# Linear attention and two feed-forward blocks on one core: clamps of the decays of seven tiles move to GpSimd, eight copies into the state move to ScalarE

## The chip, the cores and the metric

The kernel runs on one core of a Trainium2 chip. A core has five engines with a queue of instructions each: TensorE (PE in the profile, with its weight loads as PEld), VectorE (DVE), ScalarE (ACT), GpSimd (POOL) and SyncE (SP), which here issues the transfers. An engine takes its instructions strictly in the order in which they were written for it. The metric is device time in microseconds (us) of one launch.

## The reference

Batch 4, 8 heads, 768 steps, head size 48, all float32. The result of the attention, laid out as 3072 tokens by 384, goes through two feed-forward blocks.

```python
for t in range(S):
    cur = einsum('bhd,bhe->bhde', u * k[t], v[t])
    y[t] = einsum('bhd,bhde->bhe', r[t], state + cur)
    state = w[t][..., None] * state + einsum('bhd,bhe->bhde', k[t], v[t])
x = y laid out as (batch*step, heads*48)
h = x @ w_in;  x = (h * clip(h + 3, 0, 6) / 6) @ w_out            # d_ff 2048
h = x @ w_in2; s = h * softmax(h); x = layernorm(s) * g @ w_out2  # d_ff 1024
```

The decays `w` lie between 0.80 and 0.95 in the inputs. The kernel clamps them to 0.75 to 1.25 and checks on the side that none lay outside.

## The kernel before

**Tiles.** The 768 steps are cut into six chunks of 128, and a chunk of one batch is a tile: 24 tiles, numbered chunk times 4 plus batch. Tiles 0 to 3 are the first chunk. Each tile goes through six stages. `stw` clamps the decays (`wc <- w`, L451, 128x496 elements) and, on ScalarE, sums how far they lie outside. `st0` transposes `wc` and `r` on TensorE into `wt` and `rt` (L434) and runs products over time on VectorE (scans L478 and L484; `e <- rt,e`, L488). `st1` transposes `k` into `kt` and multiplies (`q <- kt,q`, L506), while GpSimd forms `z = r*k*u` (L508, L509). `st2` transposes `q` (`ktp`, L520), forms the products `pa` (L535), masks them into `am` (L543, L544, L550 for tiles 0 to 3; L553, L557 later) and sums `z` into `d` (L560 or L529). `st3` forms `kv` (L572), the tile's addition to the state, and `yt` (L582 for tiles 0 to 3; L589, L595 later), then writes the state: for tiles 0 to 3 two copies of `kv` into `s_st` (L607, 48 partitions x 192 elements each), later a sum (L605). `st4` splits the result into a high and a low part (`xh`, L641; `xl`, L642).

**PSUM.** `wt`, `rt`, `kt`, `ktp`, `pa`, `kv` and `yt` share three buffers. A matmul into a buffer waits until the last reader of what lay there is done.

**Feed-forward.** When tiles 0 to 3 are through, the first feed-forward block starts on their 512 columns in 16 slots, one for each 128 of the 2048 inner columns: 9 matmuls into `h` (L660), Relu on ScalarE (L664), a product on VectorE (`t`, L665), the high part `gh` (L666), the low part `gl` (L668, on GpSimd for the first group of 16 slots) and 9 matmuls into `y` (L680). While the first 16 slots run, VectorE also decodes the weights of each slot: five instructions on 128x768 elements (L40, L43, L50, L53, and L61 for the low part `w_l`), with two on ScalarE (L44, L60). Tiles 4 to 8 are worked in the same stretch, one for every four slots. Then the block goes through its five other groups, and the second block follows.

**Order.** For tiles 0 to 3 the order on SP and GpSimd is that of the program's text. On the other engines, and everywhere later, a scheduler sets it when the program is built, so that an edit can move instructions that it doesn't name. From tile 10 on the decays are clamped in another layout on GpSimd (L447, 128x704 elements).

Of the kernel before, what the change touches and what calls it, by code (L numbers as in the profile page):

```python
# [12 lines left out]
ACTF = mybir.ActivationFunctionType  # L13
ALU = mybir.AluOpType
# [5 lines left out]
W_LO, W_HI = 0.75, 1.25  # L20
# [247 lines left out]
def fast_path(  # L268
# [14 lines left out]
    nc = tc.nc  # L283
# [47 lines left out]
        out=causal.bitcast(F32), in_=ones, pattern=[[1, P]], compare_op=ALU.is_gt, fill=0.0, base=0,  # L331
# [96 lines left out]
    def ps_tile(nm):  # L428
        return ps_a.tile([P, 4, P], F32, tag="pa", name=nm)
# [6 lines left out]
    def stw(i):  # L436
        a = at[i]
        if i >= LATE:
            x = late["w"][:, :, 0:4 * D - 16]
            junk = atp.tile([P, HP, 4 * D - 16], mybir.dt.uint8, tag="junk", name="junk", bufs=1)  # L440
            nc.scalar.activation(
                out=junk, in_=x, func=ACTF.Relu, scale=-1.0, bias=b_lo, accum_out=chk[:, 3 * i:3 * i + 1]
            )
            nc.scalar.activation(
                out=junk, in_=x, func=ACTF.Relu, bias=b_hi, accum_out=chk[:, 3 * i + 1:3 * i + 2]
            )
            nc.gpsimd.tensor_scalar(out=x, in0=x, scalar1=W_HI, scalar2=W_LO, op0=ALU.min, op1=ALU.max)  # L447
            return
        wc = atp.tile([P, H, 64], F32, tag="wc", name="wc", bufs=1)
        flat = slice(0, H * 64 - 16)  # L450
        nc.vector.tensor_scalar(  # L451
            out=wc.rearrange("p h d -> p (h d)")[:, flat], in0=a["w"].rearrange("p h d -> p (h d)")[:, flat],
            scalar1=W_LO, scalar2=W_HI, op0=ALU.max, op1=ALU.min,
        )
        a["wc"] = wc
        junk = atp.tile([P, H, D], BF16, tag="junk", name="junk", bufs=1)
        nc.scalar.activation(
            out=junk, in_=a["w"][:, :, 0:D], func=ACTF.Relu, scale=-1.0, bias=b_lo, accum_out=chk[:, 3 * i:3 * i + 1]
        )
        nc.scalar.activation(  # L460
            out=junk, in_=a["w"][:, :, 0:D], func=ACTF.Relu, bias=b_hi, accum_out=chk[:, 3 * i + 1:3 * i + 2]
        )
# [102 lines left out]
    def st3(i):  # L565
        a = at[i]
        g, b = divmod(i, B)
        vv = a["v"].rearrange("p h d -> p (h d)")
        if g < NG - 1:
            kv = ps_tile("kv")  # L570
            for hp in range(HP):
                nc.tensor.matmul(  # L572
                    out=kv[0:DP, hp, 0:2 * D], lhsT=a["ktok"][:, hp, :], rhs=vv[:, hp * 2 * D:(hp + 1) * 2 * D],
                    start=True, stop=True,
                )
        y = ps_tile("yt")
        yf = y.rearrange("p h t -> p (h t)")[:, 0:DM]
        for hp in range(HP):
            if g == 0:
                for j in range(2):  # L580
                    h = 2 * hp + j
                    nc.tensor.matmul(  # L582
                        out=yf[:, h * D:(h + 1) * D], lhsT=a["am"][j][:, hp, :], rhs=vv[:, h * D:(h + 1) * D],
                        start=True, stop=True,
                    )
                continue
            for j in range(2):
                if g > 0:
                    nc.tensor.matmul(  # L589
                        out=y[64 * j:64 * j + D, hp, :], lhsT=a["sp"][0:DP, hp, j * D:(j + 1) * D],  # L590
                        rhs=a["e"][0:DP, hp, :], start=True, stop=False,
                    )
            for j in range(2):
                h = 2 * hp + j
                nc.tensor.matmul(  # L595
                    out=y[64 * j:64 * j + D, hp, :], lhsT=vv[:, h * D:(h + 1) * D], rhs=a["am"][j][:, hp, :],
                    start=(g == 0), stop=True,
                )
        if g < NG - 1:
            for j in range(2):  # L600
                o, f = 64 * j, D * j
                dst = s_st[b][o:o + D, :, f:f + D]
                src = kv[o:o + D, :, f:f + D]
                if g > 0:
                    nc.vector.tensor_tensor(out=dst, in0=src, in1=a["sp"][o:o + D, :, f:f + D], op=ALU.add)  # L605
                else:
                    nc.vector.tensor_copy(out=dst, in_=src)  # L607
        ys = atp.tile([P, HP, C], F32, tag="ys", name="ys", bufs=1)
        if g == 0:
            ys = ys.rearrange("p h t -> p (h t)")[:, 0:DM]  # L610
            nc.vector.tensor_tensor(out=ys, in0=yf, in1=a["av"].rearrange("p h d -> p (h d)"), op=ALU.add)
            a["ys"] = ys
            return
        for j in range(2):
            o = 64 * j
            nc.scalar.activation(out=ys[o:o + D], in_=y[o:o + D], func=ACTF.Copy)
            nc.sync.dma_start(out=x1d[i, :, j].rearrange("h d t -> d h t"), in_=ys[o:o + D])
        xf = atp.tile([P, KD, C], F32, tag="xf", name="xf")
        nc.sync.dma_start(
            out=xf, in_=x1d[i].rearrange("h j d t -> (h j d) t").rearrange("(c p) t -> p c t", p=P)  # L620
        )
        a["xf"] = xf

    def st4(i):
# [17 lines left out]
        eng.tensor_tensor(out=xl[:, :, sl], in0=xf, in1=xh[:, :, sl].bitcast(F32), op=ALU.subtract)  # L642

    stages = [stw, st0, st1, st2, st3, st4]


# [295 lines left out]
```

## Time and profile before

| | us |
|---|---|
| three runs | 813.21, 817.16, 818.41 (median 817.16) |
| the profiled execution: time | 813.55 |
| the profiled execution: span from first to last instruction | 811.8 |
| busy in the span: PE, DVE, ACT, POOL | 771.9, 539.6, 354.2, 264.5 |

Times in rows of the trace are from the span's start; a row of the timeline gives start, length, engine, line, operation, tiles out and in, shapes, and in brackets how long the engine had been idle and what ended that. Instructions of an engine overlap at their ends, so that starts lie somewhat closer than lengths. "TENSOR_TENSOR_SCAN" in the trace is the scan that the order of the program calls SCALAR_TENSOR_TENSOR on L478 and L484.

### The profile page before, as it was taken

The page shows a single profiled execution, that of the slowest core. Times are in us where ns is not written, and L with a number is a line of the kernel's source. Part 1 is how long each engine was busy: PE and PEld are TensorE (multiplying, and loading weights), DVE is VectorE, ACT ScalarE, POOL GpSimd, SP SyncE. Part 2 cuts the span into 40 slices and gives each one's busy share as a digit, 9 for nine tenths or more (in the row PEclk, how much of TensorE's full clock was granted, in tenths as well). Part 3 has the DMA queues.
Part 4 walks back from the last instruction along what each step waited for, and adds up shares of the span by engine and source line. Part 5 has one row for each costly group of instructions (what it writes and reads, how often), then busy time and mean ns, then how long its engine had stood idle before and what let it go on. Part 6 is the DMA issues. An engine that isn't in the chain of part 4 may idle for free.

```text
span 811.8 us, 12303 instructions
## 1 busy us (share of the span) xinstructions
PE 771.9 (95%) x4390; PEld 649.3 (80%) x4390; DVE 539.6 (66%) x1032; ACT 354.2 (44%) x651; POOL 264.5 (33%) x349
## 2 busy tenths in 40 slices
PE   5799888989999999999999999998999999999996
PEld 5697666668888888888888887886889999999996
DVE  5859999956666666667666663899275545555452
ACT  3325455434444544454444433554354434444342
POOL 4235635655333333333332330223032222222210
PEclk9558999999999999999999999999999999999999
DMA  9844664346444544445333212432111111111100
GB/s 183 148 92 123 157 173 136 87 94 146 101 101 101 139 101 100 101 118 117 86 80 111 71 51 61 140 102 77 39 49 40 47 43 40 45 43 42 37 21 34
DMA packets 155750, 72.56 MB, mean 89 GB/s; under 512 B 91808, under 2 KB 150304, under 8 KB 155680
## 3 DMA queue, kind: packets, MB, share of 16 engines
q1 hardware_dynamic: 153088, 66.98, 33.5%
q10 hardware_dynamic: 2592, 4.72, 1.6%
q8 instruction: 36, 0.59, 0.3%
q14 instruction: 34, 0.28, 0.1%
HBM read 58.30 MB, written 13.37 MB: 88 GB/s over the span
## 4 chain that ended last, share of the span: by engine, by line
PE 69%; DVE 5%; issue 2%; ACT 1%; DMA 1%; POOL 0%; ACTq 0%; SPq 0%; POOLq 0%; DVEq 0%
PE y L680 18%; PE h L660 17%; PE po L878 12%; PE h L851 12%; PE pt L865 3%; PE pa L535 2%; PE yt L589 2%; PE yt L595 2%; DVE dec L50 1%; PE kv L572 1%; DVE dec L53 1%; DVE t L665 1%; DMA raw<-in_moe_w_in_dram 1%; DVE raw L43 1%; PE ktp L520 1%
## 5 line engine op out<-in xcount | busy, mean ns | idle before, releaser
L665 DVE SCALAR_TENSOR_TENSOR t<-t,h 128x512 f32<-128x512 f32 x96 | 65.6, 683 | 101.7 <-ACT t L664 101.5
L664 ACT ACTIVATE t<-h,three 128x512 f32<-128x512 f32 x96 | 65.5, 682 | 133.5 <-PE h L660 133.3
L660 PE MATMUL h<-xh,w_h 128*128 128x512 f32 x288 | 114.9, 400 | 5.5 <-DVE t L665 4.1
L660 PE MATMUL h<-xh,w_l 128*128 128x512 f32 x288 | 113.9, 395 | 6.3 <-DVE w_l L61 6.2
L680 PE MATMUL y<-gh,w_h 128*128 128x512 f32 x288 | 117.2, 407 | 0.6 <-ACT gh L666 0.5
L680 PE MATMUL y<-gl,w_h 128*128 128x512 f32 x288 | 113.7, 395 | 2.5 <-POOL gl L668 2.5
L660 PE MATMUL h<-xl,w_h 128*128 128x512 f32 x288 | 113.4, 394 | 1.0 <-POOL xl L642 1.0
L680 PE MATMUL y<-gh,w_l 128*128 128x512 f32 x288 | 113.1, 393 | 0.0
L666 ACT ACTIVATE gh<-t 128x512 fp32r<-128x512 f32 x96 | 60.7, 632 | 82.7 <-DVE t L665 82.2
L553 POOL TENSOR_TENSOR am<-ident,d 128x512 f32<-128x512 f32 x40 | 50.1, 1271 | 108.0 <-PE yt L595 100.7
L660 PEld LDWEIGHTS h<-xh,w_h 128*128 128x128 f32 x288 | 54.5, 190 | 21.4 <-DVE t L665 6.6
L67 DVE TENSOR_REDUCE nm<-h 128x1 f32<-128x1024 f32 x24 | 29.4, 1225 | 62.6 <-PE h L851 62.5
L660 PEld LDWEIGHTS h<-xh,w_l 128*128 128x128 f32 x288 | 54.2, 188 | 21.0 <-DVE w_l L61 9.6
L668 DVE TENSOR_TENSOR gl<-t,gh 128x512 fp32r<-128x512 f32 x80 | 57.8, 722 | 18.8 <-ACT gh L666 17.4
L680 PEld LDWEIGHTS y<-gh,w_h 128*128 128x128 f32 x288 | 54.3, 188 | 16.7 <-issue 3.1
L878 PE MATMUL po<-w_oh,qh 128*128 128x384 f32 x192 | 67.0, 349 | 0.3 <-ACT qh L867 0.3
L680 PEld LDWEIGHTS y<-gl,w_h 128*128 128x128 f32 x288 | 54.3, 188 | 14.7 <-POOL gl L668 3.7
L878 PE MATMUL po<-w_oh,ql 128*128 128x384 f32 x192 | 65.2, 339 | 0.1
L878 PE MATMUL po<-w_ol,qh 128*128 128x384 f32 x192 | 65.0, 339 | 0.0
L660 PEld LDWEIGHTS h<-xl,w_h 128*128 128x128 f32 x288 | 54.3, 189 | 12.5 <-POOL xl L642 1.5
L680 PEld LDWEIGHTS y<-gh,w_l 128*128 128x128 f32 x288 | 54.2, 188 | 11.5
L867 ACT ACTIVATE qh<-pt 128x512 fp32r<-128x512 f32 x48 | 26.1, 595 | 79.0 <-PE pt L865 79.0
(128 smaller groups left out, 1600.4 us busy)
## 6 DMA issues: line engine op xcount, KB each, us to landing
raw<-in_moe_w_in_dram SPq DMA_DIRECT2D x24, 384.0 KB, 3.4
raw<-in_moe_w_out_dram SPq DMA_DIRECT2D x24, 384.0 KB, 4.0
r<-in_r_dram SPq DMA_DIRECT2D x24, 192.0 KB, 3.8
k<-in_k_dram SPq DMA_DIRECT2D x24, 192.0 KB, 4.1
v<-in_v_dram SPq DMA_DIRECT2D x24, 192.0 KB, 3.1
y1d<-ye ACTq DMA_DIRECT2D x18, 256.0 KB, 2.6
y<-y1d SPq DMA_DIRECT2D x24, 192.0 KB, 2.7
out_dram<-os SPq DMA_DIRECT2D x24, 192.0 KB, 1.9
```

The source lines that it names most:

```text
L67: nc.vector.tensor_reduce(out=nm, in_=h, axis=AX.X, op=ALU.max, negate=True)
L553: nc.gpsimd.tensor_tensor(out=am, in0=ident.unsqueeze(1).to_broadcast([P, HP, C]), in1=dv[:, hh, :].unsqueeze(2).to_broadcast([P, HP, C]), ...
L660: nc.tensor.matmul(out=h, lhsT=a, rhs=b, start=(j == 0), stop=(j == len(ops) - 1))
L664: nc.scalar.activation(out=t, in_=h, func=ACTF.Relu, bias=three)
L665: nc.vector.scalar_tensor_tensor(out=t, in0=t, scalar=6.0, in1=h, op0=ALU.min, op1=ALU.mult)
L666: nc.scalar.activation(out=gh, in_=t, func=ACTF.Copy)
L668: eng.tensor_tensor(out=gl, in0=t, in1=gh.bitcast(F32), op=ALU.subtract)
L680: nc.tensor.matmul(out=y_ps[g][c], lhsT=a, rhs=b, start=(m == 0 and j == 0), stop=(m == M1 - 1 and j == 2))
L851: nc.tensor.matmul(out=h[:, fs], lhsT=a[:, c, :], rhs=b_[:, c, fs], start=(j == 0), stop=(j == len(ops) - 1))
L865: nc.tensor.transpose(out=pt[:, j, :], in_=a["q"][:, m * P:(m + 1) * P], identity=ident)
L867: nc.scalar.activation(out=qh[:, ms, :], in_=pt, func=ACTF.Copy)
L878: nc.tensor.matmul(out=po, lhsT=x[:, m, :], rhs=y[:, m, :], start=(n == 0), stop=(n == 3 * M2 - 1))
```

## The change

The clamp of tiles 3 to 9 goes from VectorE to GpSimd (its two operations are swapped, to the order that the clamp of tiles 10 on has). The copies of the first chunk's `kv` into the state go from VectorE to ScalarE.

```diff
-        nc.vector.tensor_scalar(
+        eng = nc.vector if i < 3 else nc.gpsimd
+        eng.tensor_scalar(
             out=wc.rearrange("p h d -> p (h d)")[:, flat], in0=a["w"].rearrange("p h d -> p (h d)")[:, flat],
-            scalar1=W_LO, scalar2=W_HI, op0=ALU.max, op1=ALU.min,
+            scalar1=W_HI, scalar2=W_LO, op0=ALU.min, op1=ALU.max,
         )
...
                 if g > 0:
                     nc.vector.tensor_tensor(out=dst, in0=src, in1=a["sp"][o:o + D, :, f:f + D], op=ALU.add)
                 else:
-                    nc.vector.tensor_copy(out=dst, in_=src)
+                    nc.scalar.activation(out=dst, in_=src, func=ACTF.Copy)
```

The lines after the first hunk are one higher in the changed kernel. The scheduler also places other instructions anew, up to the end of the stretch with the decodes; three places follow. On VectorE, from the scan `e` of tile 2 to `q <- kt,q` of that tile (`dec` and `raw` are the weights' decode, pa_359 the products of tile 1), there stood before:

```order
L484 SCALAR_TENSOR_TENSOR e<-wt,e,ones 112x127 x4
L43 TENSOR_SCALAR raw<-raw 128x768
L488 TENSOR_TENSOR e<-rt,e 112x512
L50 SCALAR_TENSOR_TENSOR dec<-dec,raw 128x768
L451 TENSOR_SCALAR wc<-w 128x496
L53 SCALAR_TENSOR_TENSOR dec<-raw,dec 128x768
L40 TENSOR_SCALAR dec<-raw 128x768
L550 TENSOR_TENSOR am<-pa_359,causal 128x512
L61 TENSOR_TENSOR w_l<-dec,w_h 128x768
L43 TENSOR_SCALAR raw<-raw 128x768
L560 TENSOR_REDUCE d<-z 128x8
L506 TENSOR_TENSOR q<-kt,q 112x4x128
```

and in the changed kernel:

```order
L485 SCALAR_TENSOR_TENSOR e<-wt,e,ones 112x127 x4
L50 SCALAR_TENSOR_TENSOR dec<-dec,raw 128x768
L489 TENSOR_TENSOR e<-rt,e 112x512
L53 SCALAR_TENSOR_TENSOR dec<-raw,dec 128x768
L40 TENSOR_SCALAR dec<-raw 128x768
L551 TENSOR_TENSOR am<-pa_359,causal 128x512
L43 TENSOR_SCALAR raw<-raw 128x768
L61 TENSOR_TENSOR w_l<-dec,w_h 128x768
L507 TENSOR_TENSOR q<-kt,q 112x4x128
```

The clamp of tile 3 is gone, and the first L43 and the reduce (L560) stand earlier, where the two copies of tile 0 and the first L40 had stood. On VectorE around `ys` of tile 3 (L611, the last of its L611 rows), before:

```order
L451 TENSOR_SCALAR wc<-w 128x496
L550 TENSOR_TENSOR am<-pa_516,causal 128x512
L61 TENSOR_TENSOR w_l<-dec,w_h 128x768
L642 TENSOR_TENSOR xl<-px,xh 128x3x128
L607 COPY s_st_122<-kv 48x4x48 x2
L611 TENSOR_TENSOR ys<-yt,av 128x384
L50 SCALAR_TENSOR_TENSOR dec<-dec,raw 128x768
L529 TENSOR_REDUCE d<-z 128x8
L642 TENSOR_TENSOR xl<-px,xh 128x3x128
L53 SCALAR_TENSOR_TENSOR dec<-raw,dec 128x768
```

and in the changed kernel:

```order
L530 TENSOR_REDUCE d<-z 128x8
L551 TENSOR_TENSOR am<-pa_516,causal 128x512
L50 SCALAR_TENSOR_TENSOR dec<-dec,raw 128x768
L643 TENSOR_TENSOR xl<-px,xh 128x3x128
L612 TENSOR_TENSOR ys<-yt,av 128x384
L53 SCALAR_TENSOR_TENSOR dec<-raw,dec 128x768
L530 TENSOR_REDUCE d<-z 128x8
L643 TENSOR_TENSOR xl<-px,xh 128x3x128
```

One L50 and one reduce have moved from behind `ys` of tile 3 to ahead of it. On GpSimd at the end of the stretch with the decodes (`am` of tile 8, `z` of tile 9), before:

```order
L668 TENSOR_TENSOR gl<-t,gh 128x512
L553 TENSOR_TENSOR am<-ident,d 128x512 x2
L508 TENSOR_TENSOR z<-r,k 128x384
L399 MEMSET late_w 32x4x16 x2
L399 MEMSET late_r 32x4x16 x2
L399 MEMSET late_k 32x4x16 x2
L509 TENSOR_TENSOR z<-z,u_bc 128x384
L668 TENSOR_TENSOR gl<-t,gh 128x512
L502 TENSOR_TENSOR sp<-s_st_116,q 112x384
L668 TENSOR_TENSOR gl<-t,gh 128x512
L642 TENSOR_TENSOR xl<-xf,xh 128x3x128
```

and in the changed kernel:

```order
L669 TENSOR_TENSOR gl<-t,gh 128x512
L554 TENSOR_TENSOR am<-ident,d 128x512 x2
L509 TENSOR_TENSOR z<-r,k 128x384
L399 MEMSET late_w 32x4x16 x2
L399 MEMSET late_r 32x4x16 x2
L399 MEMSET late_k 32x4x16 x2
L510 TENSOR_TENSOR z<-z,u_bc 128x384
L452 TENSOR_SCALAR wc<-w 128x496
L669 TENSOR_TENSOR gl<-t,gh 128x512
L503 TENSOR_TENSOR sp<-s_st_116,q 112x384
L643 TENSOR_TENSOR xl<-xf,xh 128x3x128
L669 TENSOR_TENSOR gl<-t,gh 128x512
```

The clamp of tile 9 stands right ahead of a `gl`, and `xl` ahead of the next `gl`.

## Rows read from the trace of the kernel before

**Rows 1.** Windows: stretch, its length, busy us (instructions) by engine, granted clock, DMA.
```profile
40.00:60.00 20.00, 19.31 (x96) 18.13 (x95) 11.52 (x22) 6.22 (x14) 7.48 (x14) 0.50 0.40 90
...
80.00:100.00 20.00, 17.82 (x100) 13.36 (x100) 19.69 (x31) 10.62 (x19) 11.99 (x11) 1.00 0.63 165
...
160.00:180.00 20.00, 16.79 (x90) 12.29 (x85) 12.17 (x26) 9.05 (x17) 12.69 (x18) 0.91 0.44 102
180.00:200.00 20.00, 20.00 (x136) 16.68 (x135) 11.94 (x25) 8.46 (x15) 10.83 (x12) 1.00 0.59 139
```
**Rows 2.** Timeline of VectorE, 26 to 36 us (start, length, engine, line, operation).
```profile
26.43 0.54 DVE L43 TENSOR_SCALAR raw<-raw 128x768 int32<-128x768 int32 x1
...
28.35 0.42 DVE L451 TENSOR_SCALAR wc<-w 128x496 f32<-128x496 f32 x1
...
30.01 0.69 DVE L550 TENSOR_TENSOR am<-pa,causal 128x512 f32<-128x512 f32 x1
...
31.94 0.55 DVE L560 TENSOR_REDUCE d<-z 128x8 f32<-128x384 f32 x1
...
35.47 0.36 DVE L607 COPY s_st<-kv 48x192 f32<-48x192 f32 x1
```
**Rows 3.** Timeline of TensorE, 30 to 36 us.
```profile
30.75 1.10 PE L434 MATMUL rt<-ident,r 128*112 128x128 f32 x4 [0.51 <-DVE am L550]
...
33.15 1.81 PE L572 MATMUL kv<-v,ktok 128*112 128x96 f32 x8 [1.29 <-DVE q L506]
...
35.97 3.62 PE L582 MATMUL yt<-v,am 128*128 128x48 f32 x16 [1.01 <-POOL q L476]
```
**Rows 4.** Timeline of ScalarE, its shortest copy out of PSUM.
```profile
54.55 0.49 ACT L641 ACTIVATE xh<-px 128x384 fp32r<-128x384 f32 x1 [0.47 <-PE px L637]
```
**Rows 5.** Timeline of VectorE, 59 to 60 us.
```profile
59.42 0.56 DVE L611 TENSOR_TENSOR ys<-yt,av 128x384 f32<-128x384 f32 x1 [2.65 <-PE yt L582]
59.90 0.95 DVE L50 SCALAR_TENSOR_TENSOR dec<-dec,raw 128x768 int32<-128x768 int32 x1
```
**Rows 6.** Groups of VectorE, 60 to 165 us: count, busy us, mean ns, idle before.
```profile
L61 DVE TENSOR_TENSOR w_l<-dec,w_h 128x768 fp32r<-128x768 f32 x14 | 15.9, 1139 | 0.0
L53 DVE SCALAR_TENSOR_TENSOR dec<-raw,dec 128x768 int32<-128x768 int32 x14 | 15.7, 1121 | 0.0
L50 DVE SCALAR_TENSOR_TENSOR dec<-dec,raw 128x768 int32<-128x768 int32 x14 | 13.9, 992 | 0.0
L40 DVE TENSOR_SCALAR dec<-raw 128x768 f32<-128x768 f32 x13 | 12.5, 959 | 0.0
...
L43 DVE TENSOR_SCALAR raw<-raw 128x768 int32<-128x768 int32 x13 | 9.8, 753 | 0.0
...
L451 DVE TENSOR_SCALAR wc<-w 128x496 f32<-128x496 f32 x4 | 4.5, 1130 | 0.1
```
**Rows 7.** Timeline of GpSimd, two instructions between 105 and 117 us.
```profile
105.29 1.27 POOL L668 TENSOR_TENSOR gl<-t,gh 128x512 fp32r<-128x512 f32 x1 [3.93 <-ACT gh L666]
...
116.11 1.29 POOL L668 TENSOR_TENSOR gl<-t,gh 128x512 fp32r<-128x512 f32 x1
```
**Rows 8.** Timeline of VectorE, what started beside those two.
```profile
105.35 1.48 DVE L451 TENSOR_SCALAR wc<-w 128x496 f32<-128x496 f32 x1
...
116.57 1.65 DVE L53 SCALAR_TENSOR_TENSOR dec<-raw,dec 128x768 int32<-128x768 int32 x1
```
**Rows 9.** Timeline of GpSimd, the clamp of tile 10.
```profile
179.36 0.78 POOL L447 TENSOR_SCALAR late_w<-late_w 128x704 f32<-128x704 f32 x1 [0.43 <-ACT junk L444]
```
**Rows 10.** Timeline, GpSimd and TensorE at 169 to 171 us.
```profile
169.34 1.27 POOL L668 TENSOR_TENSOR gl<-t,gh 128x512 fp32r<-128x512 f32 x1
...
170.66 0.51 PE L680 MATMUL y<-gl,w_h 128*128 128x512 f32 x1 [1.98 <-POOL gl L668]
```
**Rows 11.** Timeline of TensorE, 16 matmuls `yt` at either clock.
```profile
18.75 1.96 PE L582 MATMUL yt<-v,am 128*128 128x48 f32 x16 [1.01 <-DVE s_st L607]
...
46.34 3.54 PE L582 MATMUL yt<-v,am 128*128 128x48 f32 x16
```

## The prediction

> **What bounds the kernel now.** I read the windows first, to see which engine limits which stretch, then the timelines of the engines around every instruction that the change names, then the groups of VectorE with their mean lengths.
>
> In the windows [rows 1] the reader is to see three kinds of stretch. From 180 us on TensorE is busy 20.00 of 20 us: nothing that VectorE or GpSimd is spared there makes the end earlier. From 80 to 100 us VectorE is busy 19.69 of 20 us and TensorE only 17.82: here VectorE is the limit, and the stretch, which begins when `ys` of tile 3 has been computed at 59.42 us [rows 5], lasts until TensorE takes over again in the window from 160 us. From 40 to 60 us TensorE is busy 19.31 us, but at a granted clock of 0.50, so at the lower level of 1.2 GHz: that stretch is a chain of tiles 1 to 3 through TensorE. Before it, up to 36 us, TensorE waits for VectorE. So a gain can come from three places: the chain up to 36 us, VectorE's work behind 59.42 us, and the hand-over to TensorE at 160 to 176 us. What is gained in them is kept, because TensorE's work behind them is fixed.
>
> **The chain of the first tiles.** Three rows of TensorE name what ended its waits [rows 3]. `rt` of tile 3 waited 0.51 us for `am` of tile 1, whose reader frees the buffer. `kv` of tile 1 waited 1.29 us for `q` of tile 2 (L506), for the same reason. `yt` of tile 1 waited 1.01 us; the profile puts it down to a memset of GpSimd, but in the order of the program that row needs the two copies of `kv`, and the second of them ended at 35.47 + 0.36 = 35.83 us [rows 2, 3].
>
> On VectorE the new order takes out of the way to `am` the clamp of tile 3 (0.42 us) and an L43 (0.54 us, which goes into the place that the first L40 had, which in turn takes the place of two copies) [rows 2]. The two are 0.96 us by their lengths, some 0.77 by their starts. On the way to `q` the reduce goes too, 0.55 us or 0.47 by starts [rows 2]: together 1.24 us. `kv` of tile 1 waited 1.29 us, so all 1.24 us can be used; `rt` ahead of it, with the 0.51 us that it waited, ends early enough: 30.24 + 1.10 = 31.34 us, against 33.15 - 1.24 = 31.91 us.
>
> The copies then run on ScalarE. No row shows a copy of 48x192 elements there. The nearest one has twice the elements and takes 0.49 us [rows 4]; the other end is what VectorE needs, 0.36 us [rows 2]. Two of them take 0.72 to 0.98 us behind the end of `kv`, against 0.87 us on VectorE (34.96 to 35.83 us), so I count no difference, with 0.15 us to either side. Behind `yt` TensorE hardly waits until 59 us [rows 1], and so the lead reaches `ys` of tile 3 whole: **-1.2 us** (-0.8 to -1.4). The clamp of tile 3 on GpSimd lies in front of a masking instruction that waits for ScalarE anyway, and tile 4's clamp is not needed before the feed-forward begins: nothing, unless `w` lands late.
>
> **Work taken from behind 59.42 us.** VectorE waited 2.65 us for `yt` of tile 3 just before its `ys` [rows 5]. The new order puts one L50 (0.95 us [rows 5]) and one reduce (0.55 us [rows 2]) ahead of that wait, which hides them; by starts that is 1.35 us less in the stretch where VectorE is the limit: **-1.35 us** (0, if their inputs come too late and they hold up `ys`, to -1.5).
>
> **The clamps in that stretch.** Four of the seven lie in it. They took 4.5 us, 1130 ns each [rows 6], but 0.42 us where GpSimd was idle [rows 2]. The reason is to be seen at 105 us: `gl` ran on GpSimd from 105.29 to 106.56 us, and the clamp that started at 105.35 us ended at 106.83 us, about its own length after that [rows 7, 8]. At 116 us an L53 did the same: 1.65 us, against a mean of 1121 ns over all 14 that includes several such waits [rows 6 to 8]. So VectorE and GpSimd hold each other up, and the wait that a clamp no longer has falls to the L50 that stands behind it. I count as saved only the bare 0.4 us, 1.6 us in all.
>
> On GpSimd a clamp costs 0.55 us if its length goes with its elements (0.78 us for 704 of them, and 496 here), and at most 0.78 us [rows 9]. In that time it holds VectorE up if a decode instruction is next. Those make 67.8 of the 105 us [rows 6], or 65%, so a clamp gives back about 0.65 x 0.55 = 0.36 us, and all four 1.4 us. What is left is **-0.2 us**. The ends: -4.5 us, if the waits go with the clamps, and 4 x (0.78 - 0.40) = +1.5 us, if each new clamp holds VectorE up for all of its 0.78 us.
>
> The Trainium skill (Perfetto Trace Analysis, Optimizing Scalar/DVE Operations) warns that the two engines share a port, so that moving work between them might not help, and SBUF — State Buffer (Who interferes with whom) says that the one that comes second waits for the whole of the other's instruction. The rows at 105 and 116 us agree with a wait to the other's end; by that rule alone the four clamps would be worth between nothing and the upper end just given, and the sum would be 1.7 us worse than mine.
>
> **The hand-over.** TensorE waited 1.98 us for the `gl` at 169.34 us [rows 10]. In the new order the clamp of tile 9 stands right ahead of that `gl`, behind the same `z`: **+0.55 us** (0 to 0.78). Its removal from VectorE brings nothing there.
>
> **Sum.** -1.2 - 1.35 - 0.2 + 0.55 = -2.2 us; with the ends of all terms, -7.4 to +1.5 us. Against the profiled execution's own time of 813.55 us this is 811.3 us. That execution lies 3.6 us below the median of the three runs, 817.16 us; the four lie at 813.21, 813.55, 817.16 and 818.41 us, with a median of 815.4 us, and I set the forecast from there: **813.2 us**.
>
> **The rivals.** (1) *Nothing.* The lead of the first tiles is lost, for example because TensorE's rise to the full clock comes no earlier and VectorE fills the time with waits at `ys`. TensorE's 19.31 busy us of 20 speak against it, since a chain without gaps passes a lead on; the many instructions that the scheduler moved speak for it. 815.4 us. (2) *The waits go with the clamps.* VectorE loses all 4.5 us of them, and the other terms stand: 815.4 - 4.5 - 1.2 - 1.35 + 0.55, about 809 us. For it: GpSimd has 8 of 20 us free [rows 1]. Against it: the L50 behind. (3) *Slower: the collisions grow.* In the stretch up to 165 us each of four clamps costs VectorE its whole 0.78 us for the 0.40 it saves, and each also shifts GpSimd's later work onto one more decode instruction, with a wait like that of the L53, 1.65 us less the 0.95 us of an undisturbed L50 of the same size, 0.70 us [rows 5, 8]: 4 x (0.38 + 0.70) = +4.3 us, and 0.78 at the hand-over, against -2.55: +2.5 us, 818 us. It decides once VectorE waits more than 0.6 us longer per tile than now. (4) *The clock.* From 40 to 60 us the granted clock is 0.50 [rows 1], and 16 matmuls `yt` take 3.54 us there and 1.96 us at the full clock [rows 11]. If the shorter waits let TensorE have the full clock for half of the 23 us from 36 to 59 us, that is 11.5 x 0.45 = -5.2 us more, about 808 us. The chain was busy there without a rise, which speaks against it.
>
> **How the numbers follow.** Forecast 0.43, nothing 0.18, waits gone 0.17, collisions grow 0.15, clock 0.07. The range leaves out most of the clock's case and the far ends of the second and third: 807 to 820 us. A difference under 1%, 8.2 us, can hardly be told from none. Faster than 809.0 us is half of the second case and most of the fourth, 0.13; slower than 825.3 us is only a far end of the third, 0.03; within 1% is 0.84.
>
> **What would show it.** In the profile of the changed kernel: `yt` of tile 1 starting near 34.7 us and `ys` of tile 3 near 58.2 us; the wait of VectorE ahead of that `ys` shorter, with an L50 in front of it; GpSimd's clamps at 0.5 to 0.8 us; the decode instructions of 60 to 165 us with the same sum of lengths, within 2 us; TensorE's wait for `gl` near 168 us of 2 to 2.5 us; and from there on the same rows, 2 us earlier. I am wrong if `ys` of tile 3 is not earlier, if the decode instructions get shorter by what the clamps had waited, or if a wait for `wc` from GpSimd shows on TensorE or on VectorE's scans.

## The result and the profile after

The changed kernel takes 807.05 us (four runs, 803.79 to 807.63) against 816.52 us for the kernel before beside it (four runs): ratio 0.9901, 95% interval 0.9872 to 0.9930 (as recorded; the two medians alone would give 0.9884). Timed again later with twelve runs it had 0.9927 (0.9902 to 0.9952). So it gains some 6 to 9 us, where the forecast of 813.2 us, made against 815.4 us, had a gain of 2.2.

In the profile the span is 6.2 us shorter (before 811.8), and TensorE's busy time hardly changed (before 771.9). These are two lines of the page of the changed kernel:

```profile
span 805.6 us, 12307 instructions
PE 772.5 (96%) x4390; PEld 656.2 (81%) x4390; DVE 531.4 (66%) x1017; ACT 355.9 (44%) x659; POOL 275.9 (34%) x356
```

The span is TensorE's busy time plus its idle time, so the gain is idle time: 811.8 - 771.9 = 39.9 us before, 805.6 - 772.5 = 33.1 us after. The windows tell where. Columns as in [rows 1]:

```profile
40.00:60.00 20.00, 19.87 (x99) 18.70 (x99) 9.69 (x16) 7.62 (x18) 10.59 (x17) 0.50 0.46 89
...
80.00:100.00 20.00, 16.81 (x107) 13.47 (x107) 19.97 (x33) 10.89 (x20) 12.82 (x10) 0.91 0.63 159
...
160.00:180.00 20.00, 19.52 (x130) 15.94 (x128) 11.70 (x23) 8.89 (x18) 11.99 (x19) 1.00 0.44 99
180.00:200.00 20.00, 20.00 (x130) 16.80 (x130) 12.34 (x24) 7.36 (x14) 7.15 (x8) 1.00 0.57 137
```

From 160 to 180 us TensorE is idle for 0.48 us and was for 3.21 us [rows 1]: this one window holds 2.7 of the 6.8 us. By the same view the rest is 1.8 us up to 60 us and 2.2 us from 60 to 160 us.

**The first tiles.** The timeline of TensorE, answering [rows 3]:

```profile
31.98 1.06 PE L434 MATMUL rt<-ident,r 128*112 128x128 f32 x4
33.95 1.81 PE L573 MATMUL kv<-v,ktok 128*112 128x96 f32 x8 [0.91 <-DVE q L507]
36.56 3.62 PE L583 MATMUL yt<-v,am 128*128 128x48 f32 x16 [0.80 <-ACT s_st L608]
```

The three waits fell from 0.51, 1.29 and 1.01 us to 0, 0.91 and 0.80 us. Still `yt` starts 0.59 us later than before. In this execution TensorE was at the lower clock, 1.2 GHz, already in `yt` of tile 0 (3.62 us, where [rows 11] has 1.96). On VectorE, answering [rows 5]:

```profile
54.88 1.34 DVE L50 SCALAR_TENSOR_TENSOR dec<-dec,raw 128x768 int32<-128x768 int32 x1
...
59.98 0.56 DVE L612 TENSOR_TENSOR ys<-yt,av 128x384 f32<-128x384 f32 x1 [3.28 <-PE yt L583]
60.45 0.95 DVE L53 SCALAR_TENSOR_TENSOR dec<-raw,dec 128x768 int32<-128x768 int32 x1
```

The L50 stands ahead of `ys` and there is still a wait of 3.28 us: it was hidden, as forecast.

**The decode stretch.** Groups of VectorE from 60 to 165 us, answering [rows 6]:

```profile
L61 DVE TENSOR_TENSOR w_l<-dec,w_h 128x768 fp32r<-128x768 f32 x14 | 18.1, 1294 | 1.8 <-ACT w_h L60 1.8
L53 DVE SCALAR_TENSOR_TENSOR dec<-raw,dec 128x768 int32<-128x768 int32 x14 | 15.4, 1101 | 0.0
L50 DVE SCALAR_TENSOR_TENSOR dec<-dec,raw 128x768 int32<-128x768 int32 x13 | 13.4, 1031 | 0.1
...
L43 DVE TENSOR_SCALAR raw<-raw 128x768 int32<-128x768 int32 x13 | 9.7, 744 | 0.0
L40 DVE TENSOR_SCALAR dec<-raw 128x768 f32<-128x768 f32 x13 | 8.9, 687 | 0.0
```

The clamps' 4.5 us are gone. The five decode lines sum to 65.5 us against 67.8, with one L50 fewer: but for that L50, 1.3 us shorter, within the 2 us that the forecast allowed. The waits moved among them, from L40 (959 to 687 ns) to L61 (1139 to 1294 ns). On GpSimd the clamps take 0.60 to 1.19 us (the forecast: 0.5 to 0.8). The 0.60 us at 62.50 us stand beside an L40 of VectorE that took 0.83 us (0.55 at 107.10 us), the 1.19 us at 105.12 us beside an L50 that took 1.53 us. Two lines of GpSimd's timeline:

```profile
62.50 0.60 POOL L452 TENSOR_SCALAR wc<-w 128x496 f32<-128x496 f32 x1 [0.20 <-PE wt L434]
...
105.12 1.19 POOL L452 TENSOR_SCALAR wc<-w 128x496 f32<-128x496 f32 x1
```

VectorE is through with the last decode, the 16th L61, earlier than the forecast's terms for this stretch allow, but can't use it. Before, and then after:

```profile
163.06 0.94 DVE L61 TENSOR_TENSOR w_l<-dec,w_h 128x768 fp32r<-128x768 f32 x1
164.03 0.69 DVE L665 SCALAR_TENSOR_TENSOR t<-t,h 128x512 f32<-128x512 f32 x1
```

```profile
157.21 1.23 DVE L61 TENSOR_TENSOR w_l<-dec,w_h 128x768 fp32r<-128x768 f32 x1 [0.78 <-ACT w_h L60]
162.56 0.55 DVE L530 TENSOR_REDUCE d<-z 128x8 f32<-128x384 f32 x1 [4.13 <-POOL z L510]
163.15 0.69 DVE L666 SCALAR_TENSOR_TENSOR t<-t,h 128x512 f32<-128x512 f32 x1
```

From the start of `ys` of tile 3 to the end of that L61 VectorE needs 98.5 us, and needed 104.6. It then waits 4.13 us for GpSimd's `z`, and the next `t` starts only 0.88 us earlier than before.

**The hand-over.** GpSimd and, last, TensorE at 164 to 168 us, answering [rows 10]:

```profile
164.58 1.29 POOL L669 TENSOR_TENSOR gl<-t,gh 128x512 fp32r<-128x512 f32 x1 [1.37 <-ACT gh L667]
165.83 0.84 POOL L503 TENSOR_TENSOR sp<-s_st,q 112x384 f32<-112x384 f32 x1
166.62 1.01 POOL L643 TENSOR_TENSOR xl<-xf,xh 128x384 fp32r<-128x384 f32 x1
...
167.68 0.51 PE L661 MATMUL h<-xl,w_h 128*128 128x512 f32 x1 [0.48 <-POOL xl L643]
```

The wait of 1.98 us for `gl` [rows 10] is gone and 0.48 us for `xl` is left. TensorE's waits from 60 to 180 us, by what ended them (total, times, longest):

```profile
PE h L661 <- DVE t L666: 3.4, 2, 3.2
PE h L661 <- DVE w_l L61: 2.1, 2, 1.5
PE h L661 <- ACT w_h L60: 1.7, 1, 1.7
PE ktp L521 <- DVE q L507: 1.1, 2, 0.6
PE px L638 <- DVE ys L612: 0.8, 1, 0.8
PE h L661 <- POOL xl L643: 0.5, 1, 0.5
```

Before, the same view had 6.2 us for `w_l`, 2.5 for `gl`, 2.0 for `wc`, 1.2 for `w_h`, 1.0 for `xl`, 0.4 for `t`. The waits for `gl` and `wc` are gone, those for `w_l` fell by 4.1 us, and 3.0 us came back in one place, `t`.

### The profile page after: what moved, and what is told of

Same layout as the page of the kernel before. It is cut to its first block, busy times and chain, and to the rows that moved or that the text cites. A ratio compares the mean times of both kernels' runs of the same rounds, so it can differ in the third digit from the quotient of the medians.

```text
span 805.6 us, 12307 instructions
## 1 busy us (share of the span) xinstructions
PE 772.5 (96%) x4390; PEld 656.2 (81%) x4390; DVE 531.4 (66%) x1017; ACT 355.9 (44%) x659; POOL 275.9 (34%) x356
## 4 chain that ended last, share of the span: by engine, by line
PE 77%; DVE 14%; issue 3%; ACT 2%; DMA 2%; SPq 1%; POOL 0%; ACTq 0%; DVEq 0%; POOLq 0%
PE y L681 18%; PE h L661 17%; PE po L879 12%; PE h L852 12%; PE pa L536 4%; PE pt L866 3%; DVE dec L50 3%; PE yt L590 2%; PE kv L573 2%; PE yt L596 2%; PE yt L583 2%; DVE w_l L61 2%; DVE raw L43 1%; DVE dec L53 1%; DVE dec L40 1%
## 5 line engine op out<-in xcount | busy, mean ns | idle before, releaser
L661 PEld LDWEIGHTS h<-xl,w_h 128*128 128x128 f32 x288 | 55.2, 192 | 12.3 <-POOL xl L643 0.9
```

Source lines behind the costliest of these rows:

```text
L661: nc.tensor.matmul(out=h, lhsT=a, rhs=b, start=(j == 0), stop=(j == len(ops) - 1))
```

## The experiments

All ratios are to the kernel before, on the same chip; one hundredth of a per cent is 0.08 us. I began with two theories: the clamps' waits go with the clamps (4.5 us), or the instructions that the scheduler moved make the gain.

**1. Copies alone.** `eng = nc.vector` for all clamps, copies on ScalarE.

> All clamps stay on VectorE, the copies of tiles 0 to 3 run on ScalarE. In the program's order an L50, an L53 and one reduce then stand ahead of VectorE's wait for `yt` of tile 3. 'The waits go with the clamps' (the four clamps of tiles 5 to 8 were worth their whole 4.5 us): only what hides in that wait is gained here, 0.95 + 1.1 + 0.55 = 2.6 us by lengths, so 1.5 to 3.5 us faster than the kernel before, ratio 0.996 to 0.998. 'The order' (what made the changed kernel fast is the instructions moved ahead of that wait): most of its 8 us, 5 to 9 us faster, ratio 0.989 to 0.994. My forecast's terms: as the first, since the clamps are worth 0.2 us by it.

Measured: 0.9945 (0.9925 to 0.9965), 4.6 us faster, with every clamp still on VectorE. That lies between the two expectations, and the interval reaches into both. TensorE is idle for 0.08 us from 160 to 180 us:

```profile
160.00:180.00 20.00, 19.92 (x123) 16.33 (x124) 11.89 (x24) 9.21 (x18) 13.76 (x19) 1.00 0.49 112
```

**2. Clamps alone.** Against the changed kernel:

```diff
-                    nc.scalar.activation(out=dst, in_=src, func=ACTF.Copy)
+                    nc.vector.tensor_copy(out=dst, in_=src)
```

> Clamps of tiles 3 to 9 on GpSimd, the copies stay on VectorE; the L50 stands behind `ys` of tile 3 again. 'The waits go with the clamps': 4.5 us for tiles 5 to 8, and up to 1 us at the start and at the hand-over: 4 to 6.5 us faster than before, ratio 0.992 to 0.995. 'The order': under 2 us faster, ratio above 0.9975. My forecast's terms: 0.2 us less for the four clamps, 0.55 more at the hand-over and at most 0.9 less in the first chain: within 1 us of before.

Measured: 1.0009 (0.9986 to 1.0032). "The waits go with the clamps" fell. At the hand-over TensorE waits 2.5 us for `xl`, and the matmul behind that wait takes 0.80 us, where the one in the changed kernel takes 0.51:

```profile
173.84 0.80 PE L661 MATMUL h<-xl,w_h 128*128 128x512 f32 x1 [2.47 <-POOL xl L643]
```

**3. Clamps of tiles 5 to 8 alone.** `eng = nc.gpsimd if 4 < i < 9 else nc.vector`, copies on VectorE.

> Only the clamps of tiles 5 to 8 on GpSimd, all else as in the kernel before; up to `ys` of tile 3 the order of VectorE is that of before, row for row. 'The waits go with the clamps': 4 to 5.5 us faster, ratio 0.993 to 0.995, and in 60 to 160 us VectorE's decode instructions keep about the 68 us that they took. 'The order': no change, ratio 0.999 to 1.001. My forecast's term: 0.2 us, no change that can be measured, the decode instructions as long as before plus the 3 us by which the clamps had waited.

Measured: 1.0057 (1.0036 to 1.0078), slower. Two groups of its VectorE, 60 to 165 us, one L50 of VectorE, and then the timelines of VectorE, GpSimd and TensorE at the hand-over:

```profile
L50 DVE SCALAR_TENSOR_TENSOR dec<-dec,raw 128x768 int32<-128x768 int32 x13 | 15.1, 1160 | 0.1
...
L558 DVE COPY_PREDICATED am<-causal,pa 128x512 f32<-128x512 int32 x8 | 5.7, 730 | 3.0 <-POOL am L554 1.8 <-PE pa L536 1.2
```

```profile
103.50 2.05 DVE L50 SCALAR_TENSOR_TENSOR dec<-dec,raw 128x768 int32<-128x768 int32 x1
```

```profile
163.19 5.03 DVE L452 TENSOR_SCALAR wc<-w 128x496 f32<-128x496 f32 x1
...
162.92 0.84 POOL L503 TENSOR_TENSOR sp<-s_st,q 112x384 f32<-112x384 f32 x1 [0.24 <-DVE q L479]
163.72 1.28 POOL L669 TENSOR_TENSOR gl<-t,gh 128x512 fp32r<-128x512 f32 x1
164.95 2.04 POOL L554 TENSOR_TENSOR am<-ident,d 128x512 f32<-128x512 f32 x2
166.96 0.99 POOL L509 TENSOR_TENSOR z<-r,k 128x384 f32<-128x384 f32 x1
...
170.37 1.01 PE L521 MATMUL ktp<-ident,q 112*128 112x112 f32 x4 [3.62 <-DVE q L507]
```

The L50 went from 992 to 1160 ns in the mean, most of it in two that stand where a clamp of 1.48 and one of 1.51 us had stood before them: they took 2.05 us each, 0.95 before. The masked copies now wait 3.0 us for what they need (0.8 before). Together that is about 4.4 us: the clamps' 4.5 us came back as other waits. And tile 9's clamp, left on VectorE, took 5.03 us beside GpSimd's row of instructions; `q` came late and TensorE waited 3.62 us.

**4. No clamps for tiles 5 to 8**, on no engine; VectorE's order is that of experiment 3.

```diff
+        if 4 < i < 9:
+            a["wc"] = a["w"]
+        else:
+            ...
```

> Leaves out the clamps of tiles 5 to 8 on any engine (wt of these tiles is transposed from w itself); otherwise as before. VectorE's order is the same, row for row, as with only these four clamps on GpSimd, so the two tell what the four clamps cost on GpSimd. 'The waits go with the clamps, and GpSimd is the one that waits': the same time as with the four clamps on GpSimd, within 1 us. My forecast's term (each clamp of GpSimd holds VectorE up by 0.36 us): 1.4 us faster than that. 'Collisions grow': more than 3 us faster than that.

Measured: 1.0063 (1.0038 to 1.0089), as in 3 within the intervals, with the same 5.03 us for tile 9's clamp. So without the four clamps on any engine nothing is gained. The intervals can't tell a cost of nothing on GpSimd from the forecast's 1.4 us. In one profile each, VectorE needs 105.1 us with them and 104.6 us without from `ys` of tile 3 to the end of the 16th L61.

**5. The order of the masked copies alone.**

```diff
-            nc.vector.tensor_reduce(out=d, in_=a["z"], axis=AX.X, op=ALU.add)
+            with tc.high_priority(offset=100):
+                nc.vector.tensor_reduce(out=d, in_=a["z"], axis=AX.X, op=ALU.add)
```

> All clamps and copies as in the kernel before; only the reduce `d` of tiles 4 and later gets a higher priority in the scheduler. VectorE's order then has, for tiles 5 to 8, the reduce early and an L61 and an L43 between the two masked copies `am`, as the changed kernel has for tiles 6 to 8; the hand-over's order is that of before. 'Order' (clamps alone gave nothing, 1.0057, and what counts is that VectorE has decode work in front of the second `am` where it waited for GpSimd): 2 to 5 us faster than before, ratio 0.994 to 0.998. 'Both are needed' (order gives nothing as long as the clamps stand on VectorE): within 1 us of before. 'The waits go with the clamps': no change.

Measured: 0.9999 (0.9979 to 1.0019). The masked copies no longer wait for `am` at all, and the 16th L61 comes at 160.94 us instead of 163.06, but from 160 to 180 us TensorE is then idle for 3.76 us, 0.6 us more than before, and its granted clock there is 0.83 (0.91 before). TensorE's idle time from 60 to 160 us fell by 1.7 us; its busy time over the span grew by 1.9 us.

**6. Clamps of tiles 5 to 9 alone**: as 3, with `i > 4`.

> As the run with only the clamps of tiles 5 to 8 on GpSimd, and the clamp of tile 9 there too. In that run tile 9's clamp on VectorE took 5.03 us at 163.19 us, beside GpSimd's work, and TensorE then waited 3.62 us for `q` and ran at a lower clock. 'The loss was that clamp': 3 to 6 us faster than that run's 818.3, so about as before, ratio 0.998 to 1.002, and TensorE's wait for `q` at 170 us under 1 us. 'The loss lies in the stretch itself' (order of 60 to 160 us): stays above 1.004. 'The waits go with the clamps': 0.993 to 0.995.

Measured: 0.9998 (0.9978 to 1.0018). The 5.03 us are gone and with them the loss of experiment 3; TensorE's wait for `q` is 0.2 us. With all five clamps off VectorE nothing is gained over the kernel before.

**7. The changed kernel without the clamps of tiles 3 to 9.**

> The changed kernel with the clamps of tiles 3 to 9 left out on every engine (wt of these tiles is transposed from w itself); VectorE's order is nearly that of the changed kernel. 'GpSimd's clamps are free': as the changed kernel, 0.988 to 0.992 of before. My forecast's term (each gives 0.36 us back to VectorE): 1.4 us faster than the changed kernel, 0.986 to 0.989. 'Collisions grow': 4 us faster than the changed kernel or more, under 0.986.

Measured: 0.9942 (0.9917 to 0.9967). Leaving them out helps no more than having them on GpSimd; it is if anything slower.

**8. Its clamps of tiles 5 to 8 done twice on GpSimd.**

```diff
+        if 4 < i < 9:
+            eng.tensor_scalar(  # the same clamp again
+                ...
```

> The changed kernel with the clamps of tiles 5 to 8 done twice on GpSimd (the same values written again); the orders of VectorE and TensorE are those of the changed kernel, row for row. 'GpSimd's clamps are free, since GpSimd does the waiting': within 1 us of the changed kernel, 0.989 to 0.992 of before. My forecast's term: 1.4 us slower than the changed kernel, about 0.992. 'Collisions grow': 4 us slower or more, 0.995 and above.

Measured: 0.9934 (0.9909 to 0.9959), which the interval can't place: by the later time of the changed kernel (experiment 9, 0.9927) "free" would be 0.9927 and the forecast's price 0.9944, and the 0.995 written for "collisions grow" lies just inside it.

**9. The changed kernel again.**

> The changed kernel once more, timed beside the other runs of this group. So far: copies alone 0.9945 of before, clamps of tiles 3 to 9 alone 1.0009, both 0.9901 from four runs. 'The copies' order does it, the clamps add only at the start': 0.990 to 0.994. 'Both work together in the stretch': 0.987 to 0.991.

Measured: 0.9927 (0.9902 to 0.9952). The twelve runs lie 8 us apart (802.85 to 810.95), and its profile shows one thing that makes executions of one kernel differ. TensorE and then VectorE in it:

```profile
45.78 1.91 PE L583 MATMUL yt<-v,am 128*128 128x48 f32 x16
...
53.46 0.56 DVE L612 TENSOR_TENSOR ys<-yt,av 128x384 f32<-128x384 f32 x1 [0.69 <-PE yt L583]
```

Here the matmuls of tile 2 already run at the lengths of 2.4 GHz, where [rows 11] has 3.54 us, and `ys` of tile 3 comes 6.52 us earlier than in the first profile of the same kernel. The span is only 3.5 us shorter, 802.1 us: the other 3 us are lost behind `ys`, where VectorE ends its 16th L61 only 3.5 us earlier.

**10. Copies of tiles 2 and 3 alone.**

```diff
+                elif b > 1:
+                    nc.scalar.activation(out=dst, in_=src, func=ACTF.Copy)
```

> Copies of tiles 2 and 3 alone on ScalarE, those of tiles 0 and 1 and all clamps on VectorE. One L50 stands ahead of VectorE's wait for `yt` of tile 3; VectorE's order for the masked copies of tiles 5 to 8 is that of before. 'Lead' (what the copies bring is only the work that the wait hides, my forecast's term): 0.9 to 1.5 us faster, ratio 0.998 to 0.999. 'Order of the rest' (the copies' gain comes mostly from the new order behind that wait): the same here, since that order isn't taken over, against 0.9945 with all copies moved. 'The copies' own time' (0.36 us each at the start): two thirds of the whole gain, 0.996 to 0.997.

Measured: 0.9995 (0.9971 to 1.0019). Half of the copies give none of the 4.6 us; "their own time" falls. For the lead it is inconclusive, since in its profile the clock rose early and the wait ahead of `ys` was 0.23 us, with nothing to hide an L50 in. TensorE is idle for 2.40 us from 160 to 180 us.

**11. The changed kernel with the clamps of tiles 3 and 4 back on VectorE**: `eng = nc.gpsimd if i > 4 else nc.vector`.

> The changed kernel with the clamps of tiles 3 and 4 back on VectorE; from tile 4 on VectorE's order is that of the changed kernel, and an L53 as well as the L50 stands ahead of the wait for `yt` of tile 3. 'The stretch decides': as the changed kernel or up to 1 us faster, 0.988 to 0.992. 'The start decides' (the clamp of tile 3 taken out of the first chain): 1 to 2 us slower than the changed kernel, 0.992 to 0.994.

Measured: 0.9929 (0.9903 to 0.9954), as the changed kernel. The clamps of the first chain don't decide either.

**12. One `t` earlier in the changed kernel.**

```diff
+        with tc.high_priority(offset=30 if n == 3 else 0):
+            nc.vector.scalar_tensor_tensor(out=t, ...)
```

> The changed kernel with one instruction given a higher priority in the scheduler: `t` of feed-forward slot 3 stands five places earlier on VectorE. In the changed kernel TensorE's longest wait behind 60 us is 3.19 us for that `t` (90.90 us). 'TensorE's waits in 60 to 180 us are what the time consists of': most of 3.2 us is gained, 2 to 3 us faster than the changed kernel. 'VectorE's sum of work is what the time consists of': no change, since VectorE does the same work and another wait takes the place.

Measured: 0.9956 (0.9929 to 0.9984). The wait of 3.19 us for `t` went, and in its place stands this line of TensorE's timeline:

```profile
93.17 1.01 PE L521 MATMUL ktp<-ident,q 112*128 112x112 f32 x4 [3.50 <-DVE q L507]
```

VectorE was full, and what stood behind `t` came late in its stead. None of the variants beats the changed kernel.

**All profiles together.** TensorE's idle time, as window length less busy time, and for the whole span:

| kernel | copies | ratio | 0 to 60 | 60 to 160 | 160 to 180 | span |
|---|---|---|---|---|---|---|
| before | VectorE | 1 | 14.1 | 11.2 | 3.2 | 39.9 |
| 2 | VectorE | 1.0009 | 12.9 | 10.5 | 2.6 | 37.5 |
| 3* | VectorE | 1.0057 | 14.1 | 13.5 | 4.1 | 43.5 |
| 4* | VectorE | 1.0063 | 14.3 | 13.2 | 4.1 | 43.3 |
| 5 | VectorE | 0.9999 | 14.0 | 9.4 | 3.8 | 38.8 |
| 6 | VectorE | 0.9998 | 13.7 | 12.3 | 2.7 | 41.2 |
| 10* | half | 0.9995 | 14.4 | 15.3 | 2.4 | 43.9 |
| after | ScalarE | 0.9901 | 12.4 | 9.0 | 0.5 | 33.1 |
| 1 | ScalarE | 0.9945 | 13.4 | 12.5 | 0.1 | 37.5 |
| 7 | ScalarE | 0.9942 | 12.5 | 11.0 | 1.5 | 36.5 |
| 8 | ScalarE | 0.9934 | 12.2 | 10.6 | 0.5 | 34.5 |
| 9* (after) | ScalarE | 0.9927 | 14.0 | 11.0 | 0.5 | 36.9 |
| 11 | ScalarE | 0.9929 | 13.4 | 10.6 | 0.0 | 35.4 |
| 12 | ScalarE | 0.9956 | 13.1 | 9.9 | 0.5 | 35.3 |

In the starred profiles the clock rose before 55 us, by the lengths of `yt` (the granted clock can't tell: it reads 1.00 up to 60 us in 1, 4, 7 and 11, though `yt` of tile 0 takes 3.62 us in all four). In 9, against the first profile of the same kernel, busy time is 7.3 us shorter and idle time 3.8 us longer; so I leave the starred ones out of the means. Of the four others with the copies on VectorE and the six on ScalarE, the mean spans are 813.5 and 808.5 us. Of those 5.0 us, 0.8 lie up to 60 us, 0.3 from 60 to 160 us, 2.6 in the window of the hand-over and 0.3 behind it; 1.0 us is busy time. The window of 160 to 180 us parts the two groups without exception, 2.4 to 4.1 against 0.0 to 1.5 us. Its granted clock does so too: 0.74 to 0.92 in the seven that keep copies on VectorE (10 keeps half), 1.00 in the seven with all of them on ScalarE, which fits the difference in busy time. A third figure parts them as well: VectorE's time from `ys` of tile 3 to the end of the 16th L61, 102.4 to 105.1 us against 98.5 to 101.7 us, though with little room between.

## Why the prediction was right in its direction and too small

807.05 us lies at the very end of the forecast's range, 807 to 820 us, and the forecast's terms make 2.2 of the 6 to 9 us. That the time fell inside is luck: the largest part of the gain came from a place where the forecast had a loss.

**The step that failed is the hand-over**, a term of +0.55 us, and the reason is how it was made: I looked at the one instruction that the diff put there, the clamp of tile 9 ahead of `gl`, and left the order around it as it was. The scheduler built another one, and the wait for `gl` that I had marked at 2 to 2.5 us is gone. Measured: -2.7 us in the first profile, -2.6 us as the mean over the kernels. It comes with the copies of tiles 0 to 3, 100 us ahead of it; experiment 1 has it with all clamps on VectorE, experiments 2 and 6 lack it with the clamps on GpSimd, and 10 with half of the copies.

**The first tiles, -1.2 us:** right in its mechanism and too large. Profiles 5 and 12 have the same clock in `yt` of tile 0 (1.96 us both); 5 has the order of before there and 12 that of the change. `yt` of tile 1 starts at 36.03 and 35.34 us, `ys` of tile 3 at 59.46 and 58.76 us: -0.7 us. TensorE's wait for `q` shrank by 0.4 us, where I had let it absorb all 1.24. That `ys` came at 59.98 us in the first profile of the change, against my mark of 58.2 us, goes with the clock: `yt` of tile 0 took 3.62 us there and 1.96 us in 12.

**The work ahead of `ys`, -1.35 us:** L50 and reduce are there, and VectorE's wait hid them in the first profile. For VectorE the term was too small: with the clamps' -0.2 us I had 1.55 us less work behind `ys`, and to the end of the 16th L61 it needed 6.1 us less in the first profile, 3.2 us less as the mean over the kernels that aren't starred. Whether TensorE's end gains by it stays open: from 60 to 160 us the groups differ by 0.3 us of idle time only.

**The four clamps, -0.2 us:** this held without the copies. Taken off VectorE with one or three of their neighbours and nothing else, they gave -0.2 and +0.7 us (experiments 6 and 2), each within 2 us. Alone they lost 4.6 us (3), and that loss went when tile 9's clamp moved too (6). Their cost on GpSimd, where I had 0.36 us each, stays open: 3 and 4 don't differ, but within intervals wider than 1.4 us. The wait fell to the L50 behind and to the masked copies, as the forecast had it for the first. Rival 2, 809 us, would have fitted the time of the changed kernel and was wrong: the 4.5 us do vanish from VectorE's rows there, but with the clamps alone off VectorE nothing is gained (2 and 6), and with all of them on it the copies alone bring 4.6 us (1). Its one profile would have confirmed the wrong rival.

**The waits for `wc`:** TensorE waited 2.0 us for the clamps themselves before, in three places. I had a wait for `wc` only as a danger of GpSimd. In 2 and 6 it is gone and other waits stand there.

**Rival 4, the clock:** 9 shows its price in one pair of profiles. An early rise was worth 6.5 us at `ys` of tile 3 and 3.5 us at the end; I had -5.2. It shows in profiles of kernels with the copies on either engine (3, 4 and 9), so nothing here makes it an effect of the change.

**What is open:** why the hand-over has no long wait in these kernels. Two rivals were not tested. It may be the order there: in every kernel with all copies on ScalarE, VectorE has a `gl` between the two masked copies of the tile there, in every other one the `gl` behind both. That is a mark of another order and not the cause, since these instructions start behind TensorE's waits (172.48 us against 167.68 in the first profile of the change, 178.69 against 175.08 before). On GpSimd `xl` stands ahead of one `gl` more in all of them, but also in 10, where TensorE still waits 2.40 us for it. Or it may be that VectorE is through with the decodes sooner, the forecast's own mechanism, seen 100 us later; against it, experiment 5 has 102.4 us there, 2.2 less than before, and yet 3.8 us of idle time at the hand-over. A kernel that changes one of the two alone wasn't run. Nor is the clamps' share in the changed kernel settled: 0.9901 and 0.9927 with both edits, 0.9945 with the copies alone, with intervals that overlap.

## What to carry to other kernels

Where a scheduler sets the order, an edit's price is not the sum of the instructions that it names: compare the order at every place where the bound passes from one engine to another, however far from the edit, and cost the waits there anew. Sum the waiting of the engine that bounds the end; removing a wait on another engine, or one wait of a full engine, mostly moves it. Before a mechanism is believed because one profile fits, run each half of the edit alone.

## What the runs showed of the hardware

An instruction of VectorE can lose to a whole row of GpSimd's. The Trainium skill (SBUF — State Buffer, Who interferes with whom) says of VectorE's two-port modes, which `tensor_scalar` can enter, that the one that issues first holds the shared ports for its whole instruction and the other blocks. The trace agrees that the clamp was held up and goes beyond that. In experiment 3 the clamp that started at 163.19 us met `sp` and was then overtaken by `gl`, both `am` and `z`, which started after it, and ended 5.03 us later with the `z`, at 168.22 against 167.95 us; experiment 4 shows the same length. So 0.42 us of work [rows 2] took 5.03 us beside five instructions. A later start doesn't always lose: in the kernel before, the same clamp started at 165.91 us, 0.04 us behind a `z`, and took 0.39 us, while the `z` took 1.31 us (1.00 at 157.73 us).

Two copies of 48x192 elements out of PSUM took 0.66 us together on ScalarE (35.80 to 36.46 us) and ended 0.70 us behind `kv`, where I had 0.72 to 0.98. On VectorE they ended 0.87 us behind it, with a reciprocal between the two.
